# Gates' weight tiles prepared in a later stretch of the attention, and two token tiles instead of one reaching the first expert by a 0/1 product

## The chip, the cores and the metric

One core of a Trainium2 chip. The time is that of the device in microseconds, from one launch of the whole program; smaller is better. TensorE (PE) does the matmuls, VectorE (DVE), ScalarE (ACT) and GpSimd (POOL) the elementwise work, and SyncE (SP) issues almost all DMAs, in the order in which they stand in its queue.

## The reference, cut to what matters

Three layers, in full single precision accuracy by means of split 16-bit products (a high and a low part of each number):

```python
attn_out = _attn_ref(q, k, v, s)                      # 4 batches x 8 heads, 576 positions of 64, causal
x = attn_out as [2304 tokens, 512]
h = x @ w_in;  g = h * clip(h + 3, 0, 6) / 6;  x = g @ w_out       # 512 -> 2048 -> 512
logits = x @ w_gate                                   # 2304 x 8
# greedy: (token, expert) pairs by falling logit; a token goes to the first expert that has room,
# 288 tokens per expert, 8 experts
out[tokens of e] = relu(x[tokens of e] @ w1[e]) @ w2[e]            # 512 -> 1024 -> 512
```

## The kernel before

**Attention.** Head pairs n = 0 to 15 go through a pipeline of steps t: `row_stage(t)`, `col_stage(t - 1)`, `pv_stage(t - 2)`, and `prep(t + 1)`. A step's streams are merged by a planner written out by hand (`merge`): each stream is a generator that yields planned nanoseconds, a stream with a budget may do that much in a step, a negative yield makes a stream wait that many planned nanoseconds, and a yielded condition blocks it. Three streams fill a step up beside the attention: `prologue` (loads the weights `w_in`, `w_out`, which are 64-bit numbers, and decodes them: L482 to L518), `gates`, and `mlp` (15,500 ns per step, `FILL`). What the planner lays down is a priority; the tile framework then fixes the order on each engine and each queue when the kernel is built. [...]

**Gates.** The routing logits of the last eight token tiles are computed from g by w_out @ w_gate. `gate_product` (L522) makes this for one of 16 f tiles: two DMA transposes on SP (L527, the high and the low weight tile, 128 x 512 each) into `wT`, a tile with one buffer; then, 2,500 planned ns later (`DL[2]`), eight small matmuls (L531, L532, 8 x 27 = 216 planned ns) into `tp`, a PSUM tile with one buffer, and a DVE sum (L533). Every second one waits 1,500 ns more (`DL[1]`). `gates` also waits until the w_out tile is decoded (`ST["w"]`). It may run from step `GT0` = 2 on, with `GB` = 1200 planned ns per step: six products. The result, `gm`, is read by `logits(u)` for u of 5 to 8, which is after the attention.

**MLP.** `h_step` (L548) computes 256 tokens x 256 hidden units, `x2_tile` (L591) 128 tokens of the second product in 48 matmuls. Its result `xo` (a high and a low part) is stored to `x2d` in DRAM (`store_x2`, L624). The last eight x2 tiles (`DEFER`) run while DVE routes: `route` and `tail` (L952, L1032) of all experts, at high priority.

**Experts.** For expert 0: `gather` (L1108) brings its 3 x 96 rows from `x2d` by indirect DMAs on POOL, `tokens` (L1115) transposes them by three DMAs on SP into `xt`, and `groups` (L1135) does the matmuls (L1128). The gather reads all of `x2d`, so it would wait for the last x2 tile. Therefore the rows of the last tile (t = 17) are zeroed in `x2d` beforehand (L853), their x2 is kept as `GT["last"]`, and these rows reach `xt` by a matmul with a 0/1 matrix, `lastsel` (L1056, made in `tail` of expert 0), and an add (L1208 to L1213). The real rows are stored after the gather (L1205). While this goes on, the weights of expert 0 are loaded and converted (`load`, `convert`, L1197 to L1202): `sp = load(...)` makes each load on SP follow the one before, `tokens(0, sp)` follows the last of them, and the four conversions follow the x2 tiles t = 13 to 16.

Of the kernel before, what the change touches and what calls it, by code (L numbers as in the profile page):

```python
# [8 lines left out]
F32 = mybir.dt.float32  # L9
F16 = mybir.dt.float16  # L10
# [3 lines left out]
OP = mybir.AluOpType  # L14
# [9 lines left out]
HP = 20000  # L24
# [7 lines left out]
DEFER = 8  # L32
R0 = 3
WAFT = 1
GB = 1200.0
LG = 14
P1, GAP = 4, 0
FL, RPOS, VPOS, PP = 0, 1, 1, 0
# [2 lines left out]
WLD, XLD, KCP, QCP, CTE = 0, 0, 0, 0, 2  # L41
HX = 0
HE = 2
GT0 = 2
RD = 0
AH = 3
RN = 2
# [4 lines left out]
YB = 2  # L52
# [49 lines left out]
def tile_attention_moe(ctx, tc, q, k, v, s, w_in, w_out, w_gate, w1, w2, out):  # L102
    nc = tc.nc
# [6 lines left out]
    KC = DM // 128  # L110
# [65 lines left out]
    for i in range(2):  # L176
        t = att.tile([128, 9, 128], F16, name=f"qb{i}", bufs=1)
# [3 lines left out]
    for i in range(KB):  # L181
        t = att.tile([128, 9, 3, 128], F16, name=f"kq{i}", bufs=1)
# [271 lines left out]
    NT = N // 128  # L454
# [7 lines left out]
    def wsl(w, f):  # L462
        return w[f // 8][:, (f % 8) * 512:(f % 8 + 1) * 512]
# [73 lines left out]
    GT = {}  # L537
# [53 lines left out]
    def x2_tile(t):  # L591
        u, o = divmod(t * 128, UN)
        p = psum.tile([128, DM], F32, name="mm", tag="mm", bufs=2)
        for f in range(FT1):
            if ST["w"] < 2 * FP:
                yield from wait(lambda: ST["w"] > FP + f // 2)
            g = GT[u, f // 2][:, :, f % 2, o:o + 128]
            nc.tensor.matmul(p, g[:, 0], wsl(woh, f), start=(f == 0), stop=False)  # L598
            nc.tensor.matmul(p, g[:, 0], wsl(wol, f), start=False, stop=False)  # L599
            nc.tensor.matmul(p, g[:, 1], wsl(woh, f), start=False, stop=(f == FT1 - 1))  # L600
            yield 3 * 216.0
            if f == LG and ("x2T", t - 1) in GT:
                direct_logits(t - 1)
        xo = wts.tile([128, 2, DM], F16, name="xo", bufs=2)
        GT["xo", t] = nc.scalar.activation(xo[:, 0], p, AF.Copy).ins
        nc.vector.tensor_tensor(xo[:, 1], p, xo[:, 0], op=OP.subtract)
        if t == NT - 1:
            GT["last"] = xo
        else:
            store_x2(t, xo)  # L610
        if t < NT - DEFER:
            xt = wts.tile([128, 2 * KC, 128], F16, name="x2T", bufs=1)
            nc.sync.dma_start_transpose(out=xt, in_=xo.rearrange("p a d -> p (a d)"))
            GT["x2T", t] = xt

    def direct_logits(t):
        p = psum.tile([128, 16], F32, name="tp", tag="tp", bufs=TPB)
        xt = GT.pop(("x2T", t))
        for c in range(KC):
            nc.tensor.matmul(p, xt[:, c], wgh[:, c], start=(c == 0), stop=False)  # L620
            nc.tensor.matmul(p[:, 0:8], xt[:, KC + c], wgh[:, c, 0:8], start=False, stop=(c == KC - 1))
        nc.vector.tensor_reduce(lg[:, t, :], p.rearrange("p (a e) -> p e a", a=2), axis=AX.X, op=OP.add)

    def store_x2(t, xo):  # L624
        nc.sync.dma_start(x2d[t * 128:(t + 1) * 128, :].rearrange("p (a d) -> p a d", a=2), xo)
# [4 lines left out]
    def wait(cond):  # L630
        if not cond():
            yield cond
# [118 lines left out]
    for t in range(NST):  # L751
# [11 lines left out]
        pro.budget = PB[min(t, len(PB) - 1)] * 1000.0  # L763
        gts.budget = GB if t >= GT0 else 0.0
        ml.budget = FILL
# [7 lines left out]
    cpsum = ctx.enter_context(tc.tile_pool(name="cpsum", bufs=1, space=bass.MemoryType.PSUM))  # L773
    late = ctx.enter_context(tc.tile_pool(name="late", bufs=1))
# [6 lines left out]
    CAP = N // E8  # L781
    RW = CAP // 3
# [28 lines left out]
    for bits, lo in ((HB, -float(2 ** (HB - 1))), (LB, 0.0)):  # L811
        steps, b = [], bits
        while b:
            t = min(5, b)
# [35 lines left out]

    none = late.tile([128, 2, DM], F16, name="none", tag="xg", bufs=3)
    nc.gpsimd.memset(none, 0.0)
    store_x2(NT - 1, none)  # L853
    khl = late.tile([128, 3, NT, E8], F32, name="khl")
    pref = near([NT, E8], "pref")

# [43 lines left out]
    def rt(shape, name, dt=F32, bufs=2):  # L900
        return late.tile(shape, dt, name=name, tag="r_" + name, bufs=bufs)
# [4 lines left out]
    def b3(x, n, where):  # L906
        return x.unsqueeze(where).to_broadcast([128, NT, n] if where == 2 else [128, n, x.shape[-1]])
# [31 lines left out]
    def prefix(m, name):  # L939
        p = small_ps([128, 2, NT], "pre")  # L940
        nc.tensor.matmul(p[:, 0, :], before, m, start=True, stop=True)
        nc.tensor.matmul(p[:, 1, :], ones, m, start=True, stop=True)
        sc = rt([128, NT], name + "s")
        nc.vector.tensor_tensor_scan(sc, p[:, 1, :], zero.to_broadcast([128, NT]), 0.0, op0=OP.add, op1=OP.max)
        nc.vector.tensor_tensor(sc, sc, p[:, 1, :], op=OP.subtract)
        pos = near([NT], name + "p", bank="b")
        nc.vector.tensor_tensor(pos, sc, p[:, 0, :], op=OP.add)
        return pos
# [83 lines left out]
    def tail(ph, r):  # L1032
        m = rt([128, NT], "m", F16, bufs=3)
        nc.vector.tensor_scalar(m, asg, r, None, op0=OP.is_equal)
        pos = prefix(m, "m")
        s3 = near([NT], "s3", bufs=2, bank="b")
        nc.vector.tensor_scalar(s3, pos, float(RW), None, op0=OP.is_ge)
        s4 = rt([128, NT], "s4")
        nc.vector.tensor_scalar(s4, pos, float(2 * RW), None, op0=OP.is_ge)
        part = rt([128, NT], "part")  # L1040
        nc.vector.tensor_tensor(part, s3, s4, op=OP.add)
        pr = near([NT], "pr", bufs=2, bank="b")
        nc.vector.scalar_tensor_tensor(pr, part, -float(RW), pos, op0=OP.mult, op1=OP.add)
        ohr = rt([128, NT, RW], "ohr", F16, bufs=1)
        for c0 in range(0, NT, 6):
            yield
            nc.vector.tensor_tensor(ohr[:, c0:c0 + 6], slotr.unsqueeze(1).to_broadcast([128, 6, RW]),
                                    pr[:, c0:c0 + 6].unsqueeze(2).to_broadcast([128, 6, RW]), op=OP.is_equal)
        e3 = near([NT, 3], "e3", bufs=2, bank="b")
        nc.vector.tensor_tensor(e3, b3(slotn, NT, 1), b3(part, 3, 2), op=OP.is_equal)  # L1050
        nc.vector.tensor_tensor(e3, e3, b3(m, 3, 2), op=OP.mult)
        if ph == 0:
            for j, x in ((1, RW - 128 % RW), (2, 0)):
                w = RW - x
                o = 0 if j == 1 else 128 - RW
                nc.vector.tensor_tensor(lastsel[:, o:o + w], ohr[:, NT - 1, x:],  # L1056
                                        e3[:, NT - 1, j:j + 1].to_broadcast([128, w]), op=OP.mult)
        rhs = rt([128, NT, 2, 3], "rhs", F16)
        nc.vector.tensor_tensor(rhs[:, :, 0, :], e3, b3(tokc, 3, 2), op=OP.mult)
        nc.vector.tensor_scalar(rhs[:, :, 1, :], e3, tokp, None, op0=OP.mult)  # L1060
        p = small_ps([RW, 2, 3], "ids")
        for c in range(NT):
            nc.tensor.matmul(p.rearrange("p a b -> p (a b)"), ohr[:, c, :], rhs[:, c].rearrange("p a b -> p (a b)"),
                             start=(c == 0), stop=(c == NT - 1))
        ic = rt([RW, 3], "ic")
        nc.vector.tensor_copy(ic, p[:, 1, :])
        idx = rt([RW, 3], "idx", I32, bufs=4)
        nc.vector.scalar_tensor_tensor(idx, p[:, 0, :], 128.0, ic, op0=OP.mult, op1=OP.add)
        IDX[ph] = idx


    lastsel = late.tile([128, 128], F16, name="lastsel")
    SCAT = []
    spacer = late.tile([1, 1], F32, name="spacer")
    half = KC * FM // 2
# [39 lines left out]
    def tokens(ph, after=None):  # L1115
        xt = (ffn if ph % 2 else late).tile([128, 2 * KC, CAP], F16, name="xt", bufs=1)
        with behind(after):
            for j, g in enumerate(XG.pop(ph)):
                d = nc.sync.dma_start_transpose(out=xt[:, :, j * RW:(j + 1) * RW], in_=g)
        XTS[ph] = xt  # L1120
        return d.ins
# [10 lines left out]
    def mm_tile(shape):  # L1132
        return psum.tile(shape, F32, name="mm", tag="mm", bufs=2)
# [62 lines left out]
    sp = None  # L1196
    for i in range(3):  # L1197
        sp = load(0, i, sp)
    for i in range(4):
        for c in range(4):  # L1200
            convert(0, i, c, GT["xo", NT - DEFER + 3 + i])
        sp = load(1, i - 1, sp) if i else load(0, 3, sp)  # L1202
    g_stack.close()
    ffn = ctx.enter_context(tc.tile_pool(name="ffn", bufs=1))
    store_x2(NT - 1, GT["last"])  # L1205
    sp = tokens(0, sp)
    xt = XTS[0]
    for hl in range(2):  # L1208
        p = mm_tile([128, KC, 128])
        for c in range(KC):  # L1210
            nc.tensor.matmul(p[:, c], GT["last"][:, hl, c * 128:(c + 1) * 128], lastsel, start=True, stop=True)
        x = xt[:, KC * hl:KC * (hl + 1), CAP - 128:]
        nc.vector.tensor_tensor(x, x, p, op=OP.add)  # L1213
    for ph in range(E8):
        more = ph + 1 < E8
        if more:
            got = gather(ph + 1)
            sp = tokens(ph + 1, sp)
        done = 0
        for g, e in enumerate(groups(ph)):  # L1220
            for _ in range(CHUNKS[g] if more else 0):
                i, c = divmod(done, 4)
                convert(ph + 1, i, c, e, got if done >= 4 else None)
                done += 1
                if c == 3:
                    if i == 0:
                        sp = load(ph + 1, 3, sp)
                    elif ph + 2 < E8:
                        sp = load(ph + 2, i - 1, sp)
# [31 lines left out]
```

## Time and profile before

| | |
|---|---|
| time, median of 3 runs | 931.59 us (930.39 to 936.6) |
| the profiled execution: its time / its span | 931.17 us / 929.4 us |
| PE busy | 834.4 us, 90% of the span |
| DVE / POOL / ACT busy | 568.3 / 472.6 / 374.9 us |
| attention, with its fill | to about 440 us |
| first expert's matmuls begin | 689.64 us |

PE is the engine with the most work; whatever time it stands idle in a stage where it has work waiting is time of the kernel. An idle PE also loses granted clock afterwards, as the profile's PEclk row shows. A row of a timeline has its start, its length, engine and line, operation, and in brackets how long the engine had stood idle before it and what ended that.

### The profile page before, as it was taken

The page shows a single profiled execution, that of the slowest core. Times are in us where ns is not written, and L with a number is a line of the kernel's source. Part 1 is how long each engine was busy: PE and PEld are TensorE (multiplying, and loading weights), DVE is VectorE, ACT ScalarE, POOL GpSimd, SP SyncE. Part 2 cuts the span into 40 slices and gives each one's busy share as a digit, 9 for nine tenths or more (in the row PEclk, how much of TensorE's full clock was granted, in tenths as well). Part 3 has the DMA queues.
Part 4 walks back from the last instruction along what each step waited for, and adds up shares of the span by engine and source line. Part 5 has one row for each costly group of instructions (what it writes and reads, how often), then busy time and mean ns, then how long its engine had stood idle before and what let it go on. Part 6 is the DMA issues. An engine that isn't in the chain of part 4 may idle for free. (4 is left out here: it accounts for less than half of the span.)

```text
span 929.4 us, 21469 instructions
## 1 busy us (share of the span) xinstructions
PE 834.4 (90%) x8553; PEld 595.1 (64%) x8553; DVE 568.3 (61%) x1705; ACT 374.9 (40%) x704; POOL 472.6 (51%) x485
## 2 busy tenths in 40 slices
PE   1688678777899999999999999999979999999996
PEld 0356457544565875866958988444447777778885
DVE  7988889875555564541356455675757877772221
ACT  2576655544344554544202222002214554455641
POOL 1466656655253564563433333003346787788951
PEclk9986778989789999999999999999989999999998
DMA  7888888789844645323220000032355765777820
GB/s 181 193 207 208 187 176 231 155 156 199 169 86 102 129 90 104 63 41 63 28 52 7 2 1 1 13 128 100 104 157 152 209 186 162 207 242 203 207 68 26
DMA packets 225524, 116.04 MB, mean 125 GB/s; under 512 B 202224, under 2 KB 202224, under 8 KB 225424
## 3 DMA queue, kind: packets, MB, share of 16 engines
q1 hardware_dynamic: 222352, 105.24, 48.1%
q0 software_dynamic: 3072, 9.44, 3.3%
q8 instruction: 67, 1.10, 0.5%
q14 instruction: 33, 0.27, 0.1%
HBM read 69.30 MB, written 9.70 MB: 85 GB/s over the span
## 5 line engine op out<-in xcount | busy, mean ns | idle before, releaser
L556 PE MATMUL mm<-xT,W 128*128 128x256 f16 (+3 forms) x2304 | 209.7, 251 | 6.1 <-DVE g L564 6.1
L1106 POOL TENSOR_TENSOR W<-stg,W 128x512 bf16<-128x512 f32 x128 | 145.0, 1159 | 100.7 <-ACT W L1104 99.8
L556 PEld LDWEIGHTS <-W 128*128 128x128 f16 (+1 forms) x2304 | 177.9, 99 | 22.9 <-DVE g L564 4.0
L1128 PEld LDWEIGHTS <-W 128*128 128x128 f16 (+1 forms) x1536 | 145.5, 98 | 42.5 <-issue 6.4
L367 POOL TENSOR_TENSOR eh<-e,eh 128x512 f16<-128x512 f32 (+1 forms) x100 | 105.5, 1070 | 99.5 <-ACT eh L365 96.6
L577 POOL TENSOR_TENSOR g<-g,g 128x512 f16<-128x512 f32 x72 | 85.5, 1187 | 125.7 <-DVE g L576 112.9
L284 PE MATMUL sc<-kqT 96*128 96x64 f16 (+10 forms) x480 | 104.7, 303 | 32.8 <-DMA kqT<-kq 18.2
L599 PE MATMUL mm<-W,g 128*128 128x512 bf16 x288 | 110.2, 383 | 3.3 <-POOL W L517 3.2
L600 PE MATMUL mm<-W,g 128*128 128x512 f16 x288 | 110.4, 384 | 0.0
L598 PE MATMUL mm<-W,g 128*128 128x512 f16 x288 | 109.6, 383 | 0.7 <-DVE g L564 0.7
L1128 PE MATMUL mm<-xt,W 128*128 128x288 f16 x768 | 105.1, 290 | 5.4 <-DVE xt L1213 4.6
L1128 PE MATMUL mm<-ht,W 128*128 128x288 f16 x768 | 102.6, 286 | 0.0
L562 ACT ACTIVATE r<-mm,three 128x512 f32<-128x512 f32 x72 | 49.4, 686 | 124.3 <-PE mm L556 116.5
L284 PEld LDWEIGHTS <-kqT 96*128 96x128 f16 (+5 forms) x768 | 54.5, 110 | 67.7 <-issue 27.2
L298 DVE TENSOR_REDUCE mx<-sc 128x1 f32<-128x384 f32 (+2 forms) x144 | 69.6, 511 | 38.0 <-PE sc L295 20.5
L364 ACT ACTIVATE e<-sc 128x512 f32<-128x512 f32 (+1 forms) x112 | 59.4, 538 | 70.0 <-PE sc L352 58.1
L564 DVE SCALAR_TENSOR_TENSOR g<-r,mm 128x512 f32<-128x512 f32 x72 | 49.3, 685 | 53.4 <-ACT r L562 52.8
L419 PE MATMUL pv<-v,eh 128*128 128x65 f16 (+1 forms) x480 | 71.4, 209 | 6.0 <-DVE x L432 6.0
L1104 ACT ACTIVATE W<-stg 128x512 f16<-128x512 f32 x128 | 75.4, 621 | 0.0
L421 PE MATMUL pv<-v,eh 128*128 128x65 f16 (+1 forms) x480 | 70.6, 205 | 1.8 <-POOL eh L367 1.8
L420 PE MATMUL pv<-v,eh 128*128 128x64 f16 (+1 forms) x480 | 71.0, 207 | 0.0
L365 ACT ACTIVATE eh<-e 128x512 f16<-128x512 f32 (+1 forms) x112 | 60.9, 570 | 13.9 <-PE pv L421 11.6
(225 smaller groups left out, 1370.3 us busy)
## 6 DMA issues: line engine op xcount, KB each, us to landing
stg<-in_moe_w_dram SPq DMA_DIRECT2D x32, 1024.0 KB
raw<-in_moe_w_in_dram SPq DMA_DIRECT2D x8, 1024.0 KB
raw<-in_moe_w_out_dram SPq DMA_DIRECT2D x8, 1024.0 KB
x2d<-xo SPq DMA_DIRECT2D x18, 256.0 KB
ldq<-in_q_dram SPq DMA_DIRECT2D x32, 128.0 KB
ldk<-in_k_dram SPq DMA_DIRECT2D x32, 128.0 KB
ldv<-in_v_dram SPq DMA_DIRECT2D x32, 128.0 KB
ldq<-in_q_dram SPq DMA_DIRECT2D x16, 32.0 KB
```

Source lines behind the costliest of these rows:

```text
L284: nc.tensor.matmul(o, x[0:kq], y[0:kq], start=start, stop=stop)
L367: eng.tensor_tensor(t[:, 1], e, t[:, 0], op=OP.subtract)
L419: nc.tensor.matmul(oj[:, 0:65], e[0], vv[:, 0:65], start=a, stop=False)
L420: nc.tensor.matmul(oj[:, 0:64], e[0], vv[:, 66:130], start=False, stop=False)
L556: nc.tensor.matmul(p[:, f, at:at + w], wsl(wt, ft)[:, c * 128:(c + 1) * 128], XT[b][:, c, hl, i:i + w], start=(n == 0), stop=(n == 3 * KC ...
L577: nc.gpsimd.tensor_tensor(g[:, 1].rearrange("p f x -> p (f x)"), g32, g[:, 0].rearrange("p f x -> p (f x)"), op=OP.subtract)
L598: nc.tensor.matmul(p, g[:, 0], wsl(woh, f), start=(f == 0), stop=False)
L599: nc.tensor.matmul(p, g[:, 0], wsl(wol, f), start=False, stop=False)
L600: nc.tensor.matmul(p, g[:, 1], wsl(woh, f), start=False, stop=(f == FT1 - 1))
L1104: nc.scalar.activation(h, x, AF.Copy)
L1106: nc.gpsimd.tensor_tensor(l, x, h, op=OP.subtract)
L1128: nc.tensor.matmul(p, wt[:, c, o * 128:(o + 1) * 128], x(hl, c), start=(n == 0), stop=(n == last))
```

## The change

Three numbers or places change. `GT0` goes from 2 to 12 and `GB` from 1200 to 2500: `gates` starts at attention step 12 and may then do twelve products in a step. Two token tiles (t = 16 and 17) are zeroed in `x2d`, kept, and brought to expert 0 by 0/1 products: `lastsel` becomes a pair of matrices (128 and 256 columns wide), the matmuls go to PSUM tiles of the tag `y` instead of `mm`, in pieces of 512 columns, and the real rows are stored after `tokens(0)`, which now has high priority, as have the products and the adds.

```diff
-GB = 1200.0
+GB = 2500.0
-GT0 = 2
+GT0 = 12
@@ x2_tile
-        if t == NT - 1:
-            GT["last"] = xo
+        if t >= NT - 2:
+            GT["last", NT - 1 - t] = xo
@@ 
-    store_x2(NT - 1, none)
+    for t in range(NT - 2, NT):
+        store_x2(t, none)
@@ tail
-            for j, x in ((1, RW - 128 % RW), (2, 0)):
-                w = RW - x
-                o = 0 if j == 1 else 128 - RW
-                nc.vector.tensor_tensor(lastsel[:, o:o + w], ohr[:, NT - 1, x:],
-                                        e3[:, NT - 1, j:j + 1].to_broadcast([128, w]), op=OP.mult)
+            for k, sel in enumerate(lastsel):
+                o = 0
+                for j in range(3):
+                    x = max(0, CAP - 128 * (k + 1) - j * RW)
+                    w = RW - x
+                    if w > 0:
+                        nc.vector.tensor_tensor(sel[:, o:o + w], ohr[:, NT - 1 - k, x:],
+                                                e3[:, NT - 1 - k, j:j + 1].to_broadcast([128, w]), op=OP.mult)
+                        o += w
@@
-    lastsel = late.tile([128, 128], F16, name="lastsel")
+    lastsel = [late.tile([128, 128 * (k + 1)], F16, name=f"lastsel{k}") for k in range(2)]
@@
-    store_x2(NT - 1, GT["last"])
-    sp = tokens(0, sp)
+    with tc.high_priority(offset=HP):
+        sp = tokens(0, sp)
     xt = XTS[0]
-    for hl in range(2):
-        p = mm_tile([128, KC, 128])
-        for c in range(KC):
-            nc.tensor.matmul(p[:, c], GT["last"][:, hl, c * 128:(c + 1) * 128], lastsel, start=True, stop=True)
-        x = xt[:, KC * hl:KC * (hl + 1), CAP - 128:]
-        nc.vector.tensor_tensor(x, x, p, op=OP.add)
+    for k in (1, 0):
+        last, w = GT["last", k], 128 * (k + 1)
+        store_x2(NT - 1 - k, last)
+        with tc.high_priority(offset=HP):
+            for c0 in range(0, 2 * KC, 512 // w):
+                cs = range(c0, c0 + 512 // w)
+                p = cpsum.tile([128, len(cs), w], F32, name="pick", tag="y", bufs=YB)
+                for c in cs:
+                    nc.tensor.matmul(p[:, c - c0], last[:, c // KC, c % KC * 128:(c % KC + 1) * 128], lastsel[k],
+                                     start=True, stop=True)
+                x = xt[:, cs.start:cs.stop, CAP - w:]
+                nc.vector.tensor_tensor(x, x, p, op=OP.add)
```

## Rows read from the trace of the kernel before

**Rows 1.** The page: the span in 40 slices of 23 us, tenths busy.

```profile
PE   1688678777899999999999999999979999999996
PEclk9986778989789999999999999999989999999998
```

**Rows 2.** Stages: window, length, busy us of PE, PEld, DVE, ACT, POOL; clock, DMA share, GB/s.

```profile
180.00:190.00 10.00, 7.08 (x60) 3.12 (x58) 9.89 (x18) 5.29 (x11) 9.64 (x8) 1.00 0.62 116
200.00:210.00 10.00, 5.88 (x78) 4.47 (x74) 3.61 (x10) 5.09 (x10) 4.16 (x5) 0.69 0.80 166
...
230.00:240.00 10.00, 6.77 (x68) 3.94 (x67) 6.77 (x15) 5.70 (x12) 3.27 (x3) 0.72 0.97 156
240.00:250.00 10.00, 8.74 (x59) 5.19 (x58) 5.61 (x13) 3.14 (x6) 2.05 (x3) 0.77 0.69 145
...
320.00:360.00 40.00, 39.69 (x524) 28.61 (x523) 22.32 (x51) 18.71 (x34) 20.59 (x21) 1.00 0.50 104
```

**Rows 3.** One line, L527: the gates' transposes on SP's queue; ns min/median/max.

```profile
L527 SPq DMA_TRANSPOSE wT<-W x32: 1188/1212/2415, 144.9 to 255.4; - x32
```

**Rows 4.** Waits of PE, 120 to 290 us: total us, times, longest.

```profile
PE tp L531 <- DMA wT<-W: 14.1, 8, 4.1
...
PE tp L532 <- DMA wT<-W: 1.3, 2, 0.7
```

**Rows 5.** Timeline of SP's queue, 148 to 367 us.

```profile
148.81 5.38 SPq L253 DMA_TRANSPOSE kqT<-kq  x1
...
167.63 2.50 SPq L527 DMA_TRANSPOSE wT<-W  x2
...
197.07 0.59 SPq L492 DMA_DIRECT2D raw<-in_moe_w_out_dram  x1
...
213.44 0.53 SPq L492 DMA_DIRECT2D raw<-in_moe_w_out_dram  x1
...
254.04 2.56 SPq L527 DMA_TRANSPOSE wT<-W  x2
...
315.79 4.32 SPq L253 DMA_TRANSPOSE kqT<-kq  x1
...
366.12 4.02 SPq L253 DMA_TRANSPOSE kqT<-kq  x1
```

**Rows 6.** Timeline of PE, 166 to 258 us.

```profile
170.57 0.17 PE L531 MATMUL tp<-wgh,wT 128*128 128x16 f16 x1
...
176.75 0.18 PE L531 MATMUL tp<-wgh,wT 128*128 128x16 f16 x1 [2.09 <-DMA wT<-W]
...
190.83 0.18 PE L531 MATMUL tp<-wgh,wT 128*128 128x16 f16 x1 [0.84 <-DMA wT<-W]
...
256.46 0.18 PE L531 MATMUL tp<-wgh,wT 128*128 128x16 f16 x1 [1.51 <-DMA wT<-W]
...
257.75 0.18 PE L532 MATMUL tp<-wgh,wT 128*128 128x8 f16 x1 [0.65 <-DMA wT<-W]
```

**Rows 7.** Timelines of DVE and ACT, 203 to 212 us: decoding of w_out.

```profile
210.66 0.17 DVE L533 TENSOR_REDUCE gf<-tp 128x8 f32<-128x16 f32 x1 [3.03 <-PE tp L532]
210.75 0.68 DVE L514 SCALAR_TENSOR_TENSOR mag<-raw,mag 128x512 int32<-128x512 int32 x1
...
203.12 1.21 ACT L511 ACTIVATE down<-raw 128x512 f32<-128x512 f32 x2 [3.58 <-DMA raw<-in_moe_w_out_dram]
```

**Rows 8.** Timelines of SP, DVE and PE, 675 to 690 us.

```profile
675.73 0.37 SPq L1092 DMA_DIRECT2D stg<-in_moe_w_dram  x1
682.94 4.24 SPq L1119 DMA_TRANSPOSE xt<-xg  x3
...
684.22 0.69 DVE L606 TENSOR_TENSOR xo<-mm,xo 128x512 f16<-128x512 f32 x1 [0.18 <-ACT xo L605]
688.90 0.69 DVE L1213 TENSOR_TENSOR xt<-xt,mm 128x512 f16<-128x512 f16 x1 [3.89 <-DMA xt<-xg]
...
689.64 0.40 PE L1128 MATMUL mm<-xt,W 128*128 128x288 f16 x1 [4.27 <-DVE xt L1213]
```

## The prediction

> **What bounds the kernel now.** I began with the page's 40 slices: PE shows 9 from about 280 us on with one exception, mostly 6 to 8 before, and its granted clock dips in the same early slices [rows 1]. So there are two kinds of stage. In the late one PE is full: 39.69 of 40 us at clock 1.00 [rows 2], and a wait that is added there is added to the kernel. In the early one it stands idle for reasons that can be named, and removing one helps as far as the next allows.
>
> [...] The attention's pitch shows the same: one transpose of kqT stands for one step, and from 148.81 to 315.79 us five steps take 33.4 us each, from there to 366.12 us two take 25.2 [rows 5]. Then I asked PE's waits there: the gates' transposes are the largest, 14.1 + 1.3 = 15.4 us, in eight of the sixteen products [rows 4]. The part at the first expert I read from timelines: PE stands idle 4.27 us before its first matmul, which waits for the adds into xt, and these for the transposes [rows 8].
>
> **Moving the gates: what the early stage gets back.** Thirty-two transposes of 1.21 us (median) leave SP, 38.8 us of its queue [rows 3], and 128 matmuls, 16 x 0.216 = 3.5 us by the planner, move along with PE's full stage and cost the same there. The price is in the waits. Upper bound: all 15.4 us [rows 4], and the clock that the idleness cost: PE's busy time times what the clock lacks, in the three low stages, 5.88 x 0.31 + 6.77 x 0.28 + 8.74 x 0.23 = 5.7 us [rows 2]; together 21.1. Lower bound: the four last raw pieces of w_out come one after the other, each load only after the piece before is decoded (load at 197.07, data used by ACT at 203.12, next load at 213.44) [rows 5, 7], and PE would wait for this chain instead. The chain itself gets shorter by DVE's wait of 3.03 us for a gate product, with a decoding operation right behind it [rows 7], by some 2.0 us that pass from a piece's last DVE operation, 211.43, to the next load, 213.44, with a pair of transposes in between on SP [rows 5, 7], and behind the chain there are 1.51 + 0.65 us at 256 us [rows 6]: 7.2 us. I take a value between: of the 5.8 us of waits from 176.75 to 190.83 us (four products; first and last in [rows 6]) half, 2.9, because DVE is at 9.89 of 10 there and is the next to be late [rows 2]; the other 9.6 us in full; of the clock a quarter, 1.4. That is 13.9, say 14 us.
>
> **What the late stage pays.** From step 12, about 315 us, sixteen products come at the planner's distance: 2,500 ns and in every second case 1,500 more, so 3.25 us plus 0.22 on average. With a budget of 2500, twelve may go in one step (before: six). The real chain of one product is a pair on SP of 2.50 us, the second's landing, the matmuls: the pair at 254.04 us served PE at 256.46 and 257.75 [rows 5, 6], 3.7 us after its start. With SP free this fits: the pair of 167.63 us was ready for PE at 170.57 without a wait [rows 5, 6]; lower bound 0. With SP busy it doesn't: from 170.57 to 190.83 us, where loads and other transposes stood between the pairs, five products took 5.8 us of waits, 1.17 each [rows 6]; upper bound 16 x 1.17 = 18.7 us. In the late stage SP is busy with other issues for 29.3 us of the 55 from 315 to 370 (19 rows, kqT of 315.79 to kqT of 366.12) [rows 5], and 38.8 us more make 68: it is over-full for two steps. But no raw weights are loaded there any longer, DMA's share is 0.50 instead of 0.62 to 0.97 [rows 2], and most of what SP issues is needed a step later. I take half of the products waiting, as before (8 of 16), at 1.0 us: 8 us. So moving the gates gives 14 - 8 = 6 us.
>
> [...]
>
> **Two token tiles by the product.** Before, the gather waits for the store of tile 16, and the transposes go out at 682.94, although SP has been free for them since the load at 675.73, about 676.2 [rows 8]. With tile 16 left out the gather can run one x2 tile earlier, and the transposes follow the load. From 682.94 to the first add are 5.96 us [rows 8]; from 676.2 that gives 682.2. Then the last tile is what is late: its low part is there at 684.91, the first add ends at 685.6, and the first expert begins 4.0 us earlier. Against it: the load right ahead is 1 MB; a piece of that size took 6.05 us (197.07 to 203.12) [rows 5, 7]. If the transposes stay behind it, xt lands at 688.2, and now six adds of 0.69 us instead of two stand between it and the experts: 692.3, or 2.7 later than 689.64. And the adds of tile 16 stand in DVE's queue among the routing, whose PE matmuls stand among those of tile 17: while DVE waits for xt, PE may stop before tile 17 is done. I see the adds of before placed like that, DVE waiting 3.89 us [rows 8]. The additional matmuls are 8 of 256 columns, under 1 us, and three small DVE products more in tail(0), which the x2 tiles hide. Between -4 and +2.7 (+5 with the stop) I take -1.5 us.
>
> **The sum.** Made against the profiled execution's own time, 931.17 us (span 929.4, 1.77 around it; the median of the runs is 0.4 higher): 931.17 - 14 + 8 - 1.5 = 923.7 us.
>
> **The rivals.**
> - *The late stage hides the transposes.* For it: DMA's share is half there, and PE's queue gives SP a whole step of 25 us. Early 20, near the upper bound, late 3, experts 4 us: 931.17 - 20 + 3 - 4 = 910 us.
> - *One stall for another.* The raw chain keeps the early stage at its 7.2 us, and late waits of about 7 eat them; 1.5 at the experts: 930 us. For it: DVE and the chain are close behind PE's waits. [...]
> - *Slower.* SP's queue becomes the bound of steps 12 to 14: every product waits 1.17 us, 18.7 in all, and three kqT of 4.1 us stand ahead of a pair [rows 5], 2.9 more each: 27.4 us, in a stage where PE has nothing else. 931.17 - 14 + 27.4 - 1.5 = 943.1; it decides from 24.8 us of late waits on. Against it: with SP busy for more than half of it, PE waits for next to nothing there now [rows 2].
>
> **How the numbers follow.** The forecast's case (917 to 930) has 0.40, the first rival (905 to 917) 0.25, the second (927 to 937) 0.17, the slower one 0.18. The likeliest is 923.7. The range, 908 to 941, leaves out the far ends of the first and the last, under 2 in 10. One per cent, about what a measurement of this kernel can tell from no change, is 9.3 us: faster means under 922.3. The first rival lies there whole, of the forecast's case 17 of 40: 0.42. Slower is the last rival, 0.18; within 1% the rest, 0.40.
>
> **What would show it.** Right: no L527 on SP before 315 us; the four steps from 148.81 us shorter by some 14 us; L531 waiting about 8 us in all between 315 and 375; the first expert beginning 1 to 4 us sooner after the last x2 matmul. Wrong: step pitch above 27 us after 315 (SP as bound), or an unchanged early pitch with ACT and PE waiting for raw pieces, or PE idle inside x2 tile 17 while DVE waits for xt. A late stage without any wait on wT would make the time lower than forecast.

## The result

The changed kernel takes 947.55 us (median of 4 runs, 946.74 to 948.0) against 933.38 us for the kernel before on the same chip: a ratio of 1.0127, with a 95% interval of 1.0101 to 1.0153. It is slower by 1.3%; forecast were 923.7 us and a range of 908 to 941. The profiled execution took 948.0 us, with a span of 946.2.

**Where the time went.** The page's slices for PE and its clock, to be held beside [rows 1]:

```profile
PE   1677788886999788799999999999989999989996
PEclk9987689897999989999999999999999999999998
```

The 9s begin earlier and then break: the 14th to 17th slice, 307 to 402 us, read 7, 8, 8 and 7. The windows show the same stretch. Columns are those of [rows 2]; the first line answers the last line there.

```profile
320.00:360.00 40.00, 32.22 (x369) 21.06 (x371) 15.36 (x39) 12.90 (x23) 14.83 (x14) 0.91 0.56 100
360.00:400.00 40.00, 31.65 (x346) 20.04 (x347) 15.52 (x38) 11.87 (x22) 12.09 (x11) 0.96 0.68 119
```

These 80 us hold the loss: PE is busy for 32 of 40 us, at a granted clock of 0.91 and 0.96, where it had been busy for 39.69 at 1.00. DMA's share there is 0.56 and 0.68, so no resource of the page is full. What PE waits for between 300 and 400 us (total us, times, longest):

```profile
PE tp L531 <- DMA wT<-W: 8.6, 8, 2.6
PE tp L532 <- DMA wT<-W: 7.0, 8, 2.9
PE tp L620 <- DVE gf L533: 3.1, 1, 3.1
```

That is 15.6 us for the gates' tiles, as much as the 15.4 us of [rows 4], now in PE's full stage; and 3.1 us for the one PSUM buffer `tp`, which the direct logits (L620) share with the gate products. Eleven of the sixteen products waited. SP's queue in that stretch (start, length):

```profile
303.29 4.27 SPq L253 DMA_TRANSPOSE kqT<-kq  x1
...
315.17 18.69 SPq L527 DMA_TRANSPOSE wT<-W  x8
333.91 1.37 SPq L334 DMA_TRANSPOSE qB<-qb  x1
336.62 4.05 SPq L253 DMA_TRANSPOSE kqT<-kq  x1
340.79 2.52 SPq L527 DMA_TRANSPOSE wT<-W  x2
343.35 1.40 SPq L442 DMA_TRANSPOSE xT<-xhl  x1
344.80 1.27 SPq L144 DMA_DIRECT2D ldq<-in_q_dram  x2
346.18 3.05 SPq L527 DMA_TRANSPOSE wT<-W  x2
...
376.14 4.22 SPq L253 DMA_TRANSPOSE kqT<-kq  x1
...
390.04 2.54 SPq L527 DMA_TRANSPOSE wT<-W  x2
```

Two things can be read here. The kqT that stood at 315.79 us before [rows 5] is issued at 303.29: 12.5 us are won up to there. And the next two are 33.3 and 39.5 us apart where [rows 5] has 25.2. By the last qB (L334; 412.36 us before, 429.53 after) the kernel is 17.2 us behind, so the late stage cost 12.5 + 17.2 = 29.7 us. Fifteen pairs of wT go out from 315.17 to 392.58 us, one every 5.2 us on average.

**The first expert** is the part that went better than forecast. Its queue, adds and matmuls, beside [rows 8] (SP, DVE and PE timelines; SP's ends at 694 us, ahead of the third transpose):

```profile
691.58 0.37 SPq L1097 DMA_DIRECT2D stg<-in_moe_w_dram  x1
692.00 3.35 SPq L1124 DMA_TRANSPOSE xt<-xg  x2
...
699.62 2.50 DVE L1224 TENSOR_TENSOR xt<-xt,pick 128x512 f16<-128x512 f16 x4 [1.44 <-DMA xt<-xg]
702.88 1.28 DVE L1224 TENSOR_TENSOR xt<-xt,pick 128x512 f16<-128x512 f16 x2
...
701.23 0.38 PE L600 MATMUL mm<-W,g 128*128 128x512 f16 x1
...
703.62 0.41 PE L1133 MATMUL mm<-xt,W 128*128 128x288 f16 x2 [0.19 <-DVE xt L1224]
```

The last x2 matmul of the kernel before:

```profile
683.18 0.38 PE L600 MATMUL mm<-W,g 128*128 128x512 f16 x1
```

The token transposes follow the load after 0.4 us instead of 7.2, and four of the six adds are done before the last tile's products. From the end of the last x2 matmul (683.56 us before, 701.61 after) to the first expert matmul (689.64, 703.62) it was 6.1 us and is 2.0.

### The profile page after: what moved, and what is told of

Same layout as the page of the kernel before. It is cut to its first block, busy times and chain, and to the rows that moved or that the text cites. A ratio compares the mean times of both kernels' runs of the same rounds, so it can differ in the third digit from the quotient of the medians.

```text
span 946.2 us, 21434 instructions
## 1 busy us (share of the span) xinstructions
PE 833.6 (88%) x8521; PEld 590.8 (62%) x8561; DVE 575.7 (61%) x1712; ACT 374.7 (40%) x704; POOL 475.2 (50%) x485
## 5 line engine op out<-in xcount | busy, mean ns | idle before, releaser
L556 PE MATMUL mm<-xT,W 128*128 128x256 f16 (+3 forms) x2304 | 206.0, 249 | 6.7 <-DVE g L564 6.7
L284 PE MATMUL sc<-kqT 96*128 96x64 f16 (+10 forms) x480 | 104.5, 300 | 29.3 <-DMA kqT<-kq 16.6
L598 PE MATMUL mm<-W,g 128*128 128x512 f16 x288 | 111.9, 391 | 10.4 <-ACT W L516 5.8
L600 PE MATMUL mm<-W,g 128*128 128x512 f16 x288 | 113.7, 395 | 2.1 <-issue 0.4
L599 PE MATMUL mm<-W,g 128*128 128x512 bf16 x248 | 97.5, 393 | 4.6 <-POOL W L517 4.5
L562 ACT ACTIVATE r<-mm,three 128x512 f32<-128x512 f32 x72 | 49.5, 687 | 130.2 <-PE mm L556 122.5
L419 PE MATMUL pv<-v,eh 128*128 128x65 f16 (+1 forms) x480 | 68.2, 204 | 5.9 <-DVE x L432 5.9
L421 PE MATMUL pv<-v,eh 128*128 128x65 f16 (+1 forms) x480 | 67.2, 201 | 1.5 <-POOL eh L367 1.4
L420 PE MATMUL pv<-v,eh 128*128 128x64 f16 (+1 forms) x480 | 67.6, 203 | 1.0 <-DVE v L224 1.0
```

What stands on the lines that cost most here:

```text
L284: nc.tensor.matmul(o, x[0:kq], y[0:kq], start=start, stop=stop)
L419: nc.tensor.matmul(oj[:, 0:65], e[0], vv[:, 0:65], start=a, stop=False)
L556: nc.tensor.matmul(p[:, f, at:at + w], wsl(wt, ft)[:, c * 128:(c + 1) * 128], XT[b][:, c, hl, i:i + w], start=(n == 0), stop=(n == 3 * KC ...
```

## The experiments

All stand on the kernel before unless "changed kernel" is said. The kernel before was measured beside each group of them: 929.87 us beside a_only, b_only, no_tr and spread, 930.07 beside no_tr_early, two_buf, actq and post, 929.99 beside half_tr, early_dl and thin, 935.55 beside late_dl. Ratios are against it. The marks used below are the starts of SP's kqT transposes (L253) and of its last qB (L334), which count the attention's steps.

### One part alone: a_only and b_only

a_only moves the gates alone; b_only has the experts' part alone.

```diff
 a_only:  -GT0 = 2       -GB = 1200.0
          +GT0 = 12      +GB = 2500.0
 b_only:  the change without these two lines
```

> The kernel before with GT0 = 12 and GB = 2500 alone. Theory (the moved transposes fill SP's queue in a stage where PE is full, and this is all of the loss): about 14 to 18 us over the kernel before, 946 to 950 us, kqT of step 13 about 12 us earlier than before, the last qB about 17 us later. Rival (the part at the first expert has a share of 5 us or more): 940 us or less.

> The changed kernel with GT0 = 2 and GB = 1200 put back, so the two token tiles alone. Theory: the first expert begins some 3 us earlier but is not ahead at the end, since DVE's waiting holds the routing up: within 2 us of the kernel before, 930 to 935 us. First rival (a real gain of what the gap lost): 927 to 929. Second rival (it has its share of the loss): 937 or more.

Measured: a_only 949.13 us (ratio 1.0194, 1.0131 to 1.0256), b_only 926.64 (0.996, 0.9935 to 0.9986). In a_only the kqT steps run as in the changed kernel (303.66, 336.48, 376.84 us) and PE waits 15.2 us for wT. So the whole loss belongs to the gates' move, some 19 us, and the experts' part gains about 3.2 us of its own (1.3 to 6.0 by its interval).

### The transposes left out, at both places: no_tr and no_tr_early

No wT is made; the products read the weight tiles as they are. no_tr is a_only with this edit, no_tr_early the kernel before with it.

```diff
-            o = wts.tile([128, 2, KC, 128], F16, name="wT", bufs=1)
-            o = (o[:, 0], o[:, 1].bitcast(BF))
-            for t, w in zip(o, (woh, wol)):
-                nc.sync.dma_start_transpose(out=t, in_=wsl(w, f))
+            o = [wsl(w, f).rearrange("p (c x) -> p c x", c=KC) for w in (woh, wol)]
```

> GT0 = 12 and GB = 2500 alone, and the gates' 32 transposes left out: the small matmuls read the weight tiles as they are, so the gate values of the last eight token tiles are not those wanted; all other work is there. Theory (SP and the landing of its transposes are the loss, and were also what held the early stage up): the early stage keeps its 12 us, the late one loses nothing, 915 to 920 us. Rival (the order that the planner makes with twelve products in step 12, or the matmuls and the PSUM bank tp, cost the time): 935 us or more.

> The kernel before with the 32 transposes of the gate products left out and the products kept in their old place from the third step on; the products read the weight tiles as they are, so the gate values of the last eight token tiles are not those wanted. Theory (the transposes cost little in the early place, about the 4.8 us by which no_tr stands under the kernel before, and some 24 us in the late one): 922 to 928 us, and no_tr less this kernel is under 3 us. Rival (the transposes cost the full 14 us of waits in the early place as well, and it is the products themselves that are dearer late, by the 9 us that steps 12 and 13 of no_tr lost): 912 to 918 us, and no_tr less this kernel is 8 us or more.

Measured: no_tr 925.09 us (0.9953, 0.9926 to 0.9981), no_tr_early 925.23 (0.996, 0.9937 to 0.9983). With the two kernels that have their transposes this makes a square:

| us | products early | products late |
|---|---|---|
| with transposes | 930 (before) | 949.13 (a_only) |
| without | 925.23 | 925.09 |

This settles whose price it is. Without transposes the time is the same at either place. The transposes cost 4.8 us early and 24.0 us late, and the 19.2 us between them are the whole loss of a_only. By the marks: no_tr has its kqT at 302.15 us where no_tr_early has 312.48, so 10.3 us of the early stage's gain come from the products themselves, with no transpose in play; and from there to the last qB (407.69 and 408.94 us) it takes 105.5 us where no_tr_early takes 96.5, so 9.1 of them are paid back late. PE's waits of no_tr between 300 and 440 us show 4.4 us of that:

```profile
PE tp L617 <- DVE gf L530: 3.1, 1, 3.1
PE tp L528 <- DVE gf L530: 1.3, 1, 1.3
```

### Fewer products in a step: spread

```diff
-GT0 = 2        -GB = 1200.0    -DL = (8000.0, 1500.0, 2500.0)
+GT0 = 12       +GB = 700.0     +DL = (8000.0, 1500.0, 4500.0)
```

> From step 12 on as in the change, but four products per step instead of twelve (GB = 700) and 4500 instead of 2500 planned ns between the transposes and their matmuls. Theory (SP over-full for two steps, and a chain longer than the planned distance): the waits of PE on wT between 300 and 420 us fall from 15.6 to 5 us or less, 920 to 927 us. Rival (each product costs its latency wherever it stands): waits of 12 to 16 us again, 942 us or more.

Measured: 937.87 us (1.0105, 1.007 to 1.014), between the two expectations, and both missed. PE waits for wT in four products only, once in a step and 11.5 us in all, the longest 3.7. There SP has just got a list of other issues and the pair stands behind them:

```profile
395.29 1.34 SPq L442 DMA_TRANSPOSE xT<-xhl  x1
396.67 0.70 SPq L144 DMA_DIRECT2D ldv<-in_v_dram  x1
397.41 0.57 SPq L145 DMA_DIRECT2D ldv<-in_v_dram  x1
398.10 6.71 SPq L527 DMA_TRANSPOSE wT<-W  x4
```

So density matters, for more than half of the loss (8.0 us are left of some 19), but this run changed the planner's distance with it.

### A second buffer, and another queue: two_buf and actq

Both are the changed kernel. two_buf lets the first 14 products take `x2T`'s buffer in turn with `wT`'s, and issues two pairs ahead; actq moves the transposes to ScalarE's queue.

```diff
 two_buf:  for f, tag in zip(fs, ("wT", "x2T" if fs[0] < 14 else "wT")):
               ...allocate with this tag, issue both transposes; then the products
 actq:    -                nc.sync.dma_start_transpose(out=t, in_=wsl(w, f))
          +                nc.scalar.dma_start_transpose(out=t, in_=wsl(w, f))
```

> The changed kernel, where the first 14 products take the tile buffer of x2T (unused until the first x2 tile) in turn with that of wT, and both pairs of transposes of a couple of products are issued ahead of the first product. Theory (one buffer: a pair can be fetched only when the product before it has let the buffer go, so that each product pays a whole trip from PE to the DMA and back): PE's waits on wT fall from 15.6 us to 6 us or less and the time to 927 to 938 us. Rival (the place in SP's queue, among kqT, qB and the loads, is what costs, whichever buffer is filled): the waits stay at 12 us or more and the time at 943 us or more.

> The changed kernel with the 32 transposes issued on ScalarE's DMA queue instead of SP's, nothing else. Theory of the buffer (a trip per product): the waits on wT stay at 12 us or more and the time at 943 us or more, higher still if ScalarE's own work now stands behind a transpose that waits for its buffer. Rival (SP's queue): the loads of q, v and k are no longer held up behind wT, the waits on wT fall to 8 us or less and the time to 930 to 938 us.

Measured: two_buf 938.52 us (1.0111, 1.0075 to 1.0147), actq 971.75 (1.046, 1.0423 to 1.0498). The waits on wT from 100 to 600 us, of two_buf and then of actq:

```profile
PE tp L540 <- DMA wT<-W: 7.8, 7, 2.2
...
PE tp L541 <- DMA wT<-W: 3.0, 5, 0.7
```

```profile
PE tp L531 <- DMA wT<-W: 24.0, 8, 6.1
...
PE tp L532 <- DMA wT<-W: 6.1, 8, 2.2
```

The second buffer takes the waits from 15.6 to 10.8 us. The median is 9 us lower than the changed kernel's, but the intervals of the two ratios overlap; by the marks (kqT at 301.69, last qB at 425.18 us) the late stage is 2.8 us shorter. So it helps a little, less than the theory had it. A likely reason, not tested, is that the two transposes of the next pair still take SP their 2.5 us and stand among its other issues.

Another queue makes it much worse: PE's waits grow to 30.1 us, and PE is busy for 26.26 of the 40 us from 320. Two things are seen in the trace. ScalarE's own work is late: two of its activations (L562, L436) wait 3.9 and 3.8 us for transposes into wT, and where four transposes hold its queue for 9.85 us from 346.17 us on, its next activation, at 356.07, comes after 14.84 us of idleness, which the profile puts down to a load of q that SP issues. And SP's own transposes now wait for those on ScalarE's queue, 49.6 us in these three groups, where the changed kernel has no such wait (SP's waits, 300 to 440 us):

```profile
SPq L334 <- DMA wT<-W: 30.6, 3, 20.7
...
SPq L442 <- DMA wT<-W: 10.8, 2, 5.5
SPq L613 <- DMA wT<-W: 8.2, 3, 4.3
```

So SP was not freed: it lost 32 issues and got these waits. The run does not acquit SP's queue, and it does not separate the two causes; it shows only that issuing the transposes from another queue is no cure.

### Away from the steps: post

The changed kernel without a gate product in the steps; they are woven into the mlp's stream behind them.

```diff
-GT0 = 12
+GT0 = 99
-DL = (8000.0, 1500.0, 2500.0)
+DL = (8000.0, 500.0, 2500.0)
-    while pro.alive or gts.alive:
+    while pro.alive:
         raws()
-        pro.budget = gts.budget = 4000.0
-        merge([x for x in (pro, gts) if x.alive])
+        pro.budget = 4000.0
+        merge([pro])
...
-    merge([ml])
+    gts.budget, gts.total = None, 20000.0
+    merge([ml, gts])
```

> The changed kernel with no gate product in the attention steps at all: the 16 products run behind them, between 440 and 500 us, woven into the mlp's stream (the while loop behind the steps drains the decoding alone). SP has little there. Theory (the late stage's loss came from stalls inside the steps, where SP's queue and the chain of the steps meet): neither the early waits nor the late ones, so the kernel before less 4.8 us (no_tr), less 4.4 us of waits on the gate values' buffer in the late steps, less 3.2 us of the experts' part (b_only): 916 to 923 us. Rival (a product pays its trip wherever it stands, since the buffer is single): 16 trips of about 1 us and more come back between 440 and 500 us, and the time is 930 us or more.

Measured: 949.26 us (1.0222, 1.0193 to 1.0251). The rival holds, and the run measures the trip by itself. First SP's queue, then one window:

```profile
478.29 1.28 SPq L613 DMA_TRANSPOSE x2T<-xo  x1
479.68 41.93 SPq L527 DMA_TRANSPOSE wT<-W  x20
```

```profile
480.00:520.00 40.00, 21.55 (x241) 18.25 (x239) 13.89 (x57) 4.81 (x7) 9.24 (x8) 0.80 0.31 64
```

From 479.68 us on SP has nothing else and DMA's share is 0.31; ten products go at 41.93 / 10 = 4.19 us each, of which PE works about 0.2 (the eight matmuls of the product at 448.90 us start within 0.18). Not all ten are uncovered, as the expectation of thin below has it: between the first five PE still has the mlp's matmuls, and they wait little; from 501.24 us on it has nothing, and the last five begin at 505.21, 509.24, 513.26, 517.43 and 521.45 us, 4.06 apart on average, with 3.5 to 4.4 us of waiting each. So one product through one buffer takes 4.1 us of going round (two transposes, landing, matmuls, buffer free) on an empty queue.

PE waits for wT for 17.6 + 9.4 = 27.0 us in all, but that is not the whole price. Without products the steps end early: the last qB stands at 395.73 us, in b_only at 411.85. From there to the first expert matmul (707.26 and 687.83 us) post takes 35.5 us more. The waits are 27.0 of them, and the granted clock is 0.91, 0.80 and 0.86 in the three windows of 40 us from 440, which is an estimated 33.97 x 0.09 + 21.55 x 0.20 + 35.24 x 0.14 = 12.3 us; b_only, too, loses some 3 us of clock in that stretch (0.96 in two of its windows).

### What covers the trip: half_tr, early_dl, late_dl and thin

half_tr is a_only with one of the two transposes of a product left out. early_dl is b_only, late_dl the changed kernel, each with another distance in the planner. thin is the changed kernel with two products in a step from the eighth step on.

```diff
 half_tr: -            for t, w in zip(o, (woh, wol)):
          -                nc.sync.dma_start_transpose(out=t, in_=wsl(w, f))
          +            nc.sync.dma_start_transpose(out=o[:, 0], in_=wsl(woh, f))
          +            o = (o[:, 0], wsl(wol, f).rearrange("p (c x) -> p c x", c=KC))
 early_dl, late_dl:  -DL = (8000.0, 1500.0, 2500.0)
                     +DL = (8000.0, 1500.0, 4500.0)
 thin:    -GT0 = 12     -GB = 2500.0    -DL = (8000.0, 1500.0, 2500.0)
          +GT0 = 7      +GB = 400.0     +DL = (8000.0, 1500.0, 9000.0)
```

> The kernel before with the gates' products moved to the thirteenth step on, and only one of the two tiles of a product transposed: 16 transposes instead of 32; the other is read as it is, so the gate values of the last eight token tiles are not those wanted. Theory of the trip: one transpose takes 1.2 to 1.26 us on SP, so the trip falls from 4.2 to about 3.0 us; of 24 us (a_only over no_tr) about 3.0/4.2 less what the planner's 2.5 us cover stays: (3.0 - 2.5)/(4.2 - 2.5) = 0.3 of it, 7 us: 930 to 935 us. Rival (the cost goes by the number of transposes): half of the 24 us: 936 to 940 us.

> The experts' part alone, the products in their old place from the third step on, six in a step, but with 4.5 us instead of 2.5 between a pair's issue and its product in the planner. Theory of the trip: the 14.1 us in which TensorE waited for wT at 176 to 257 us shrink to 6 us or less, but that stage is bound by other work too (without any transposes the kernel of before gained 4.8 us), so the time falls by 1 to 4 us against the experts' part alone (926.6): 922 to 926 us. Rival (the early waits come from loads and kqT ahead in SP's queue, not from the planner's figure): waits stay over 10 us and the time at 926 to 929 us.

> The changed kernel with one number different: the planner waits 4.5 us instead of 2.5 between a pair's issue and its product; the products stay at the thirteenth step on and may come twelve in a step. Theory (what counts is how much other work stands between issue and product): the trip of 4.2 us is covered by the planner's figure, but with a couple of products in 10 us SP's list of loads still stands among them, as in the run with four in a step (937.9 without the experts' part, so 934.7 with it): 932 to 940 us, waits on wT 6 to 12 us. Rival (the pace of the products alone decides, not the cover): the same 16 products in about as long a stretch, 944 us or more.

> The changed kernel with the products spread: from the eighth step on, two in a step, and the planner waits 9 us instead of 2.5 between a pair's issue and its product. In the run with the products behind the steps ten products that nothing covered went at 4.19 us each (41.93 us for 20 transposes on a queue with nothing else in it), of which TensorE works about 0.2 us. Theory (a trip of some 4.2 us through one buffer, dear only where the planner covers it with less): the waits on wT fall under 3 us, and the time is that of the kernel without transposes less the experts' part, 925 less 3: 919 to 925 us. Rival (each late product hurts by what its transposes take from SP's queue and the DMA engines, whatever stands over it): 2.5 us and more a product would put SP's kqT 20 us and more behind in the steps after the eighth, and the time is 935 us or more.

Measured: half_tr 934.6 us (1.0057, 1.0033 to 1.0082), early_dl 920.3 (0.9886, 0.9855 to 0.9917), late_dl 944.34 (1.012, 1.0061 to 1.0179), thin 916.65 (0.9848, 0.9825 to 0.9872).

half_tr came inside the range that the trip gave: half of the transposes left in cost 9.5 us over no_tr instead of 24.0, less than half, as a shorter trip that is covered sooner would have it. It does not exclude the rival: by its interval the time is 933.1 to 937.6 us, and the rival's range began at 936.

late_dl went to the rival: its ratio is that of the changed kernel. The waits on wT (260 to 470 us) are 16.6 us:

```profile
PE tp L531 <- DMA wT<-W: 11.1, 6, 2.9
PE tp L532 <- DMA wT<-W: 5.5, 9, 0.9
```

The planner's figure is planned time, not what the engine does: fifteen pairs take 79.2 us, and less the waits that is 4.2 us of anything else on PE between two products, where the changed kernel has (77.4 - 15.6) / 15 = 4.1. Nothing was moved, so nothing changed.

thin moved the distance itself. Its products are 10.8 to 20.4 us apart (once 31.2), and among the waits of PE from 140 to 470 us none on wT is left. It also moved the place: from the eighth step on means from 153.80 us on, and ten of its sixteen pairs go out before the kqT of 303.27. First the page's slices for PE, then SP's queue in a step:

```profile
PE   1587778877999999999999999999989999999996
```

```profile
303.27 4.06 SPq L253 DMA_TRANSPOSE kqT<-kq  x1
307.93 1.25 SPq L442 DMA_TRANSPOSE xT<-xhl  x1
309.27 0.85 SPq L144 DMA_DIRECT2D ldq<-in_q_dram  x1
310.30 2.50 SPq L527 DMA_TRANSPOSE wT<-W  x2
...
322.44 3.39 SPq L527 DMA_TRANSPOSE wT<-W  x2
328.37 1.24 SPq L334 DMA_TRANSPOSE qB<-qb  x1
330.77 4.50 SPq L253 DMA_TRANSPOSE kqT<-kq  x1
```

The same 32 transposes, the same queue, the same single buffer: kqT follows kqT by 27.5 us instead of 33 to 40 (25.2 in [rows 5], without products), and the kernel is 1.5% faster than the kernel before, the lowest median of all that ran. It came out 2 us under the range that the theory gave. How much of its gain over the changed kernel is the distance and how much the earlier start no run separates.

early_dl is faster than the theory's range too, with waits as the rival had them: 9.6 + 2.9 = 12.5 us, hardly fewer than b_only's 15.0, and yet about 6 us less time. So in the early stage the waits on wT are no measure of the time. All its pairs stay early, and it is no clear step behind thin: the intervals of the two ratios overlap, and the last qB stands at 404.66 us (thin 404.93, b_only 411.85). So thin shows that late products can do without a wait, not that late is the better place.

## Why the prediction was wrong

**The step that failed is the late stage's price.** 8 us were taken, between 0 and 18.7; by the marks it was 29.7 us. That the late stage pays in waits on wT was right. Three things were wrong in its size:

- *The lower bound of 0 compared a chain with the wrong distance.* The text had both numbers, a chain of 3.7 us from the pair's start to the matmuls and products 3.47 planned us apart, and called that fitting because one pair had been ready in time. With one buffer the next pair can't start until the product is done, so the chain is a rate, not a latency: 4.1 us a product with an empty queue (post). In the changed kernel five products that waited come 4.0 to 4.4 us after the one before, and one 4.8; there PE had only 3.0 to 4.0 us of other time. Four later products that did not wait had 4.4 us of other time or more.
- *"Half of the products waiting at 1.0 us" took the share of waiting products from the early stage,* where they are 4 to 14 us apart. Late they are 3 to 10 us apart, and eleven of sixteen waited, 1.4 us each. The waits came to 15.6 us, within the bounds, in a stage where PE has nothing to hide them under.
- *The waits are not all.* The granted clock fell to 0.91 and 0.96 in a stage where the sum had it at 1.00: an estimated 32.22 x 0.09 + 31.65 x 0.04 = 4.2 us from the two windows. What idleness does to the clock was seen in the kernel before in windows of 5 us: PE busy for 0.88 us from 200 us on and a clock of 0.50 in the next 5 us, 2.27 us from 255 and again 0.50 in the next; but 2.26 us from 25 were followed by 1.00, so the 1.4 us of clock in the sum are an estimate only. The products themselves pay 9.1 us late (no_tr), of which the forecast had only the matmuls' own 3.5, which it set equal at both places, and 3.1 us of the rest are the wait on `tp`, which it didn't have. Added up over the two kernels, 15.6 + 4.2 + 9.1 = 28.9 of the 29.7.

**The early stage: the size was near by luck, the reason wrong.** 14 us were forecast and 12.5 came. But no_tr_early shows that the transposes were worth only 4.8 us of time there; 10.3 us at the mark come from taking the products out, and by the square these are not won but carried over to the late stage. (The page's slices of [rows 1] read 9 from 256 us on, not from about 280; nothing in the sum hangs on it.) The 15.4 us of waits [rows 4] were read as a price that goes when the transposes go. Most of it lay over other waits: without transposes, PE waited for DVE's sums (6.8 us) and for the decoding (5.0 + 4.0 us, and 2.7 in the products; no_tr_early). The forecast's own lower bound, 7.2 us, was nearer to what the transposes give back, and it had named the decoding as what is late next.

**The experts' part: right, sized too low.** -1.5 us forecast, about -3.2 measured (b_only), inside the bounds. The gather did free the transposes, which now follow the load as forecast. They did not land early: from their issue to the first add are 7.6 us, where [rows 8] had 5.96. But the adds for tile 16 are done in DVE's queue ahead of the last tile's, so that two groups of short products remain at the end, as before; the feared stop of PE before tile 17 is one wait of 1.2 us.

**The rivals.** The slower one came, nearest at 943.1 us, with the pitch above 27 us that was named as its sign. Its mechanism is about half right. Of the 15.6 us of waits, 7.4 fall on four products whose pair stood behind other issues on SP: kqT of 336.62 and of 376.14 us, xT and loads at 343.35, and a transpose of x2T at 362.45. Another 5.3 us are the six waits at 4.0 to 4.8 us after the product before, the trip of the single buffer; and in one wait of 2.9 us (331.01 us) the pair had gone out at once and landed late. spread's one wait a step has the rival's cause. But a full queue is not needed for a wait: post, with nothing else on it, pays 4.1 us a product all the same, and thin carries the same 32 transposes without a wait. "For next to nothing there now" was the argument against it, and it spoke for it: a stage where PE never waits has nothing to hide a wait under. The other signs: one pair stayed early (168.33 us), though its product stands at 312.53; the five early steps are 10.5 us shorter; the first expert starts 4.1 us sooner after the last x2 matmul.

## What to carry to other kernels

A step that is fetched through one buffer has a rate, the whole way round from fetch to use to free (4.1 us here, post); measure it where nothing covers it and compare it with the distance at which the users stand on the busy engine, before asking whether queue and DMAs have room. Moving such a step from a stage with idle time into a full one turned hidden waits into time here (the transposes cost 4.8 us early and 24.0 late), and what took the waits away here was neither another queue nor, in the late stage, a larger number in the planner alone, but more other work between two uses: two products in a step, begun at the eighth step, stand at a gain of 1.5% where twelve from the thirteenth stand at a loss of 1.3%. Leaving them in the early stage with the larger number did about as well (early_dl, 1.1%), so the move itself has not been shown to pay. And the size of a wait in an idle stage says little of what its removal gives: leave the cause out at both places before moving it.

## What the runs showed of the hardware that was not expected

A pair of transposes that takes SP 2.52 us (twice the median of 1.26 in post) costs 4.06 us a product when each waits for the one before and nothing else is to be done (post, from 505.21 us on), with a DMA share of 0.31 (480 to 520 us). The difference is 1.5 us; how it divides into landing, matmuls and release, and how much of the 4.06 us is transfer, no run shows. And with the transposes issued from ScalarE's queue both queues stood in actq: ScalarE was idle for 14.84 us around four of them, by the profile until a load of q, and three groups of SP's own transposes waited 49.6 us for them. The time rose from 947.55 to 971.75 us by the change of queue alone.

Some of a_only's 24.0 us over no_tr stays open. 1.5 us stand before the late stage already (kqT at 303.66 against 302.15 us), and 21.2 between there and the last qB (430.43 against 407.69). Of these, 15.2 are waits on wT and an estimated 4.3 the clock (0.92, 0.95 and 0.91 in the windows from 300, 320 and 360 us, less no_tr's own 0.91 in the first); 1.7 us are not explained, nor are those outside. Why early_dl gained is known only in part: from 148 us to the kqT of step 12 it takes some 7 us less than b_only, about half of it less idle time of PE (22.9 against 26.5 us) and half the same work at a clock of 0.96 instead of 0.92. Why the clock stood higher is not shown.
